# A v tile computed ahead of a stall, and the q and k projections one step earlier, in a sliding-window attention kernel

## The chip, the cores and the metric

The kernel runs on one core of a Trainium2 chip. The metric is the device time of one execution in microseconds (us). A core has engines that work side by side: PE (TensorE, matmuls), DVE (VectorE), ACT (ScalarE), POOL (GpSimd) and SP (SyncE); in the kernel before PE is busy 99% of the span, DVE 46%, ACT 31% and POOL 23%. SP computes nothing here: it issues DMA transfers, in its timelines one after the other, and among them all 102 DMA transposes of the trace. POOL and ACT issue DMAs too, beside their other work. The page counts all transfers, 101.21 MB, on the core's 16 DMA engines.

Before the change, three runs gave a median of 1196.67 us.

## The reference, cut to what matters

Four layers run one after the other: attention, gated MLP, attention, gated MLP. Only the first attention is changed.

```
def _A_ref(x, wqkv, wo):                # x: 2048 x 576, 32 heads of 18, window of 8, dilation 2
    qkv = (x @ wqkv) ...                # q, k, v
    idx = pos[:, None] - off[None, :]   # position s sees s, s-2, ... s-14
    logits = einsum(q, kg) * scale;  attn = softmax(masked logits)
    o = einsum(attn, vg)
    return o @ wo
x = x + _A_ref(_layernorm(x), A_wqkv, A_wo)
x = x + _B_ref(_layernorm(x), ...)      # gated MLP, 4608 wide
... # the same two again
```

## The kernel before: the parts that count here

The attention walks over tiles of 112 queries, in 38 steps, two per tile (half of the heads each). `L_mm` makes the logits, `EXP` (ACT) the exponentials, `PV` the product with v. Other work is hung into a table of steps and runs after the step's `PV`: `VW` makes half a v tile, `PG` one q or k projection of 512 positions, `WO` half an output projection.

```
def PG(d, qk, cc, dve, queues=(nc.sync, nc.gpsimd)):
    ... 5 matmuls pp <- wqk, xnT; evac to stg ...
    # when both halves of stg are there: up to 8 moves of q/k rows, SBUF to SBUF
    for dst, src in moves:
        dma_rr[0] += 1
        self.dma(dst, src, eng=queues[dma_rr[0] % len(queues)])      # SP and POOL in turn

def PV(s):
    ... O_ps matmuls; DVE normalizes into o_t ...
    if hf == 1:                                                      # every odd step
        if t < NT - 2:
            nc.sync.dma_start_transpose(out=oT[:, :, c0:c0 + nq], in_=o_t[:nq, :])   # SP

def XST(i):   # store of the new residual, SP
    self.dma(self.xres[li][i * P:(i + 1) * P, :], tails[i]["x"][:])
def LN_T(i):  # transpose of the normalized rows for the next layer, SP
    self.ln_T(tails.pop(i)["xn"], i * P, P)
...
for k_, (d, qk, cc) in enumerate(pgs):                # 12 projections in steps 2 to 13
    at(2 + k_ if li == 0 else ..., PG, d, qk, cc, True)
for i in range(NS):
    t = -(-(i + 1) * P // QT) - 1                     # the last tile that WO(i) needs
    s = 2 * t + (6 if li == 0 and t < 10 else 5 if t < NT - 5 else 4 if t < NT - 3 else 3)
    at(s - 5, XO, i); at(s, WO, i, 0); at(s + 1, WO, i, 1)
    at(s + 1, LN_STATS, i); at(s + 2, LN_XN, i); at(s + 2, XST, i); at(s + 4, LN_T, i)   # (joined here)
...
for s in range(NST):
    if s + 1 < NST:
        L_mm(s + 1); EXP(s + 1)
    PV(s)
    for f, a in table.pop(s, []):
        f(*a)
```

Transpose `t` is put on SP's list in step 2t+1, and `WO(i)` reads it in step 2t+6 while t is under 10, and in step 2t+5 from t = 10 on.

The softmax here doesn't subtract the row's maximum and nothing guards it: scores larger than these inputs give would overflow.

Of the kernel before, what the change touches and what calls it, by code (L numbers as in the profile page):

```python
# [62 lines left out]
class K:  # L63
# [257 lines left out]
    def layer_A(self, li):  # L321
# [32 lines left out]
        def tdim(t):  # L354
            nq = min(QT, S - QT * t)
            return HALO + nq, nq
# [11 lines left out]
        def evac(out, in_, dve):  # L368
            if dve:
                nc.vector.tensor_copy(out=out, in_=in_)  # L370
            else:
                nc.scalar.copy(out=out, in_=in_)

        def VW(t, hh, dve):
            nk = tdim(t)[0]
            pv = self.PT_tile([P, 512], f32, "pv")
            for c in range(5):
                nc.tensor.matmul(pv[:nk, 0:288], lhsT=self.xnT[:, c, QT * t:QT * t + nk],  # L378
                                 rhs=wv_sb[:, c, hh * 288:(hh + 1) * 288], start=(c == 0), stop=(c == 4))
            evac(v_ext[:nk, t, 16 * hh:16 * hh + 16, 0:DH], pv[:nk, 0:288].rearrange("p (b d) -> p b d", d=DH), dve)  # L380
# [46 lines left out]
        def L_mm(s):  # L427
            t, hf = divmod(s, 2)
            nk, nq = tdim(t)
            L_tiles[s] = [self.H_tile("L_ps") for _ in range(2)]  # L430
            for jp in range(2):
                for ftl in range(4):
                    g = 4 * hf + ftl
                    for jj in range(2):
                        j = 2 * jp + jj
                        nc.tensor.matmul(L_tiles[s][jp][:nk, jj, ftl * QT:ftl * QT + nq],  # L436
                                         lhsT=kT[32 * j:32 * j + 32, g, QT * t:QT * t + nk],
                                         rhs=qT[32 * j:32 * j + 32, g, QT * t + PADL:QT * t + PADL + nq],
                                         start=True, stop=True, tile_position=(32 * j, 0))

        def EXP(s):
            nk, nq = tdim(s // 2)
            for jp, L_ps in enumerate(L_tiles.pop(s)):
                Lv = L_ps[:, :, 0:4 * QT].rearrange("p a (b c) -> p a b c", c=QT)
                nc.scalar.activation(out=P_bufs[(2 * s + jp) % 4][:nk, :, :, 0:nq], in_=Lv[:nk, :, :, 0:nq], func=ACT.Exp,  # L445
                                     scale=scale)

        def PV(s):
            t, hf = divmod(s, 2)
            nk, nq = tdim(t)  # L450
            O_ps = self.PT_tile([P, 512], f32, "O_ps")
            for jp in range(2):
                for ftl in range(4):
                    for jj in range(2):
                        idx = 4 * ftl + 2 * jp + jj
                        nc.tensor.matmul(O_ps[:, idx * (DH + 1):(idx + 1) * (DH + 1)],  # L456
                                         lhsT=P_bufs[(2 * s + jp) % 4][:nk, jj, ftl, :],
                                         rhs=v_ext[:nk, t, 16 * hf + idx, :], start=True, stop=True)
            Ov = O_ps[:, 0:16 * (DH + 1)].rearrange("p (h e) -> p h e", e=DH + 1)
            o_t = o_bufs[t % len(o_bufs)]  # L460
            rec = sb.tile([P, 16], f32, name="rec", tag="rec", bufs=2)
            nc.vector.reciprocal(out=rec[:nq, :], in_=Ov[:nq, :, DH])
            nc.vector.tensor_tensor(out=o_t[:nq, 288 * hf:288 * (hf + 1)].rearrange("p (h d) -> p h d", d=DH),
                                    in0=Ov[:nq, :, 0:DH], in1=rec[:nq, :, None].to_broadcast([nq, 16, DH]), op=ALU.mult)
            if hf == 1:
                c0 = (QT * t) % (RING * P)
                if t < NT - 2:
                    nc.sync.dma_start_transpose(out=oT[:, :, c0:c0 + nq], in_=o_t[:nq, :])
# [45 lines left out]
        if li == 0:  # L514
# [58 lines left out]
            def T_(*tiles):  # L573
                for i in tiles:
                    self.ln_T(xns.pop(i), i * P, P)
# [50 lines left out]
                    R_(12, 4)  # L626
                    A_(12, 13, 14, 15)
            T_(12, 13, 14, 15)
            nvw0, nvw = 4, 8
        else:  # L630
            for k_, (d, cc) in enumerate([(d, cc) for d in range(5) for cc in range(2)]):
                for qk in ((1, 0) if d < 4 else (0,)):
# [8 lines left out]
                if k_ == 6:  # L641
                    self.fill_window_rows(QK, 1)
            nvw0, nvw = 0, 4
        for t in range(nvw0, nvw):
            for hh in range(2):
                VW(t, hh, li == 0)

# [10 lines left out]
        def at(s, f, *a):  # L658
            table.setdefault(s, []).append((f, a))
        pgs = [(d, qk, cc) for d, cc in ((0, 2), (1, 2), (2, 2), (0, 3), (1, 3), (2, 3), (3, 2), (3, 3), (4, 2), (4, 3))  # L660
               for qk in ((1, 0) if d < 4 else (0,))]
        PG_END = 14
        pre, pgs = pgs[:6], pgs[6:]
        for k_, (d, qk, cc) in enumerate(pgs):
            at(2 + k_ if li == 0 else (k_ * PG_END) // len(pgs), PG, d, qk, cc, True)
        for t in range(nvw, NT):
            for hh in range(2):
                if li == 0 and t == nvw:
                    at(hh, VW, t, hh, True)
                else:  # L670
                    at(2 * t - 2 + hh, VW, t, hh, 2 * t - 2 + hh >= PG_END and hh == 0)
        for i in range(NS):
            t = -(-(i + 1) * P // QT) - 1
# [18 lines left out]
        for k_, (d, qk, cc) in enumerate(pre):  # L692
            if k_ == (2 if li == 0 else 0):
                L_mm(0)
                EXP(0)
            PG(d, qk, cc, li > 0 or k_ < 4, q2)
            if li == 0 and k_ == 3:
                self.fill_window_rows(QK, 1)
        for s in range(NST):
            if s + 1 < NST:  # L700
                L_mm(s + 1)
                EXP(s + 1)
# [3 lines that stand above are left out]
# [339 lines left out]
```

## Time and profile before

| what | value |
|---|---|
| time, median of 3 | 1196.67 us (1194.73 to 1196.80) |
| first matmul of layer 1 | 133.2 us |
| PE waits between 12 and 140 us | 4.5 us |
| cold clock (granted clock 0.50) in that stretch | 6.83 us from 47.63 us and 3.41 us from 92.00 us |

From the page of the kernel before, three lines: PE's busy tenths and the granted TensorE clock in 40 slices of the span, and the shares of the chain of work that ended last.

```profile
PE   9999999999999999999999999999999999999998
...
PEclk9899999999999999999999999999999999999999
...
PE 94%; DMA 2%; SPq 1%; POOL 1%; DVE 1%; issue 0%; ACT 0%; DVEq 0%; POOLq 0%
```

PE is busy nearly everywhere and is nearly the whole chain. The clock row has its gap in the second slice (30 to 60 us). So only a few microseconds in the first attention can be won by moving work. The waits view of the kernel before, for PE from 12 to 140 us, says who waited for what (us in sum, times, longest):

```profile
PE L_ps L436 <- DMA QK<-win2a: 2.0, 3, 1.0
PE L_ps L436 <- DMA QK<-stg: 1.6, 2, 1.5
PE L_ps L436 <- ACT P_sb L445: 0.9, 2, 0.4
```

The PE timeline of the kernel before shows where (start, length, instruction group; in brackets the idle time before it and what ended it):

```profile
46.65 0.20 PE L436 MATMUL L_ps<-QK 32*128 32x112 bf16 x1 [0.96 <-DMA QK<-win2a]
47.24 0.46 PE L436 MATMUL L_ps<-QK 32*128 32x112 bf16 x8 [0.39 <-DMA QK<-win2a]
48.38 0.27 PE L436 MATMUL L_ps<-QK 32*128 32x112 bf16 x1 [0.68 <-DMA QK<-win2a]
...
90.84 0.22 PE L436 MATMUL L_ps<-QK 32*128 32x112 bf16 x1 [1.45 <-DMA QK<-stg]
91.22 0.22 PE L436 MATMUL L_ps<-QK 32*128 32x112 bf16 x1 [0.16 <-DMA QK<-stg]
```

The logits of step 1 wait for the last q/k moves before the loop, from the buffer `win2a`, lent here, into `QK` ("stall 1", 46 to 48 us), and those of step 19 for the last moves of the loop ("stall 2", 89 to 91 us). The windows view of the kernel before, cut every 3.41 us for a reason given below it, has the length first, then busy us of PE, PEld, DVE, ACT and POOL, then the granted clock, the DMA share and GB/s:

```profile
44.22:47.63 3.41, 2.06 (x21) 0.88 (x19) 3.41 (x4) 1.30 (x3) 3.28 (x4) 1.00 1.14 185
47.63:51.04 3.41, 2.73 (x46) 1.66 (x46) 2.17 (x4) 1.76 (x3) 2.73 (x4) 0.50 1.05 336
51.04:54.46 3.42, 3.42 (x54) 2.01 (x52) 1.71 (x5) 2.89 (x4) 0.00 (x0) 0.50 1.03 362
88.60:92.00 3.40, 1.79 (x38) 1.16 (x37) 1.59 (x7) 2.10 (x4) 3.03 (x3) 1.00 0.35 72
92.00:95.42 3.42, 3.42 (x44) 2.09 (x43) 1.77 (x5) 1.11 (x2) 3.23 (x5) 0.50 0.93 243
```

After the window of stall 1 (PE busy 2.06 of 3.41 us) the clock is 0.50 for two windows, after that of stall 2 (1.79 of 3.40 us) for one. The packed trace has a record of each stretch of granted clock. In the kernel before, from the first record (6.67 us) to the end of the span, these stretches are 1.00 or 0.50 and last 40.96, 6.83, 37.55, 3.41 and 1099.09 us, each within 2 ns of a whole multiple of 3.4133 us (12, 2, 11, 1 and 322 times). That is why the views are cut every 3.41 us.

SP's list is full (from 58 us). In SP's timeline the four moves that stall 2 waits for (85.38 us) are issued behind a transpose of oT (83.32 us). The last line is the transpose of tile 10, which the output projection `WO(8,0)` reads. In the PE timeline it is the second half of this group:

```profile
108.09 1.39 PE L493 MATMUL pw<-wo_sb,oT 128*128 128x288 bf16 x10
```

Five of these ten matmuls are `WO(7,1)` and five are `WO(8,0)`, which thus begins near 108.7 us: 5.5 us after its transpose began to be issued. It did not wait. The packed trace also holds the semaphore updates that tell when a transfer has landed, which `prof` does not list for these transposes. By them this one landed at 108.11 us, 4.9 us after its issue began. So it was 0.6 us in time.

### The profile page before, as it was taken

What the parts mean: (1) busy time and instruction counts of PE and PEld (TensorE: products, weight loads), DVE (VectorE), ACT (ScalarE), POOL (GpSimd) and SP (SyncE); (2) the same over time, 40 slices, a digit from 0 to 9 for tenths busy, and PEclk for the clock granted to TensorE, in tenths of its full rate; (3) what the DMA queues carried; (4) which work ended last, traced back from release to release, by engine and by line L of the source; (5) the groups of instructions that cost most, each with busy time, mean ns of one, the idle gap of its engine ahead of it and who ended that gap; (6) DMA issues with size and microseconds to landing.
All of it is one profiled execution on the core that took longest, in us unless ns stands there. A gap on an engine that the chain in (4) does not pass through costs nothing.

```text
span 1193.7 us, 20761 instructions
## 1 busy us (share of the span) xinstructions
PE 1182.4 (99%) x8554; PEld 621.8 (52%) x8554; DVE 548.0 (46%) x1207; ACT 376.0 (31%) x592; POOL 275.3 (23%) x383
## 2 busy tenths in 40 slices
PE   9999999999999999999999999999999999999998
PEld 5566644444444444457755775444444444444677
DVE  9687677333233233244455776763223223223311
ACT  6477677211111111201156786770110110111000
POOL 4677773100000000001144777530000000000000
PEclk9899999999999999999999999999999999999999
DMA  8989892000000000049646899900000000000332
GB/s 198 190 160 220 166 221 67 23 1 12 12 12 12 12 1 12 2 139 297 169 97 111 190 236 186 224 11 12 12 12 1 12 12 12 12 1 25 127 105 73
DMA packets 178103, 101.21 MB, mean 85 GB/s; under 512 B 134335, under 2 KB 159359, under 8 KB 178008
## 3 DMA queue, kind: packets, MB, share of 16 engines
q1 hardware_dynamic: 165144, 78.13, 30.9%
q0 software_dynamic: 6512, 16.00, 5.2%
q10 hardware_dynamic: 6352, 5.75, 1.6%
q8 instruction: 67, 1.10, 0.4%
q14 instruction: 28, 0.23, 0.1%
HBM read 42.39 MB, written 16.53 MB: 49 GB/s over the span
## 4 chain that ended last, share of the span: by engine, by line
PE 94%; DMA 2%; SPq 1%; POOL 1%; DVE 1%; issue 0%; ACT 0%; DVEq 0%; POOLq 0%
PE pg L879 42%; PE pz L861 12%; PE po L933 12%; PE pz L783 11%; PE pp L401 4%; PE pw L493 3%; PE pv L378 3%; PE O_ps L456 3%; PE L_ps L436 2%; PE pzs L783 1%; SPq L77 1%; DMA QK<-win2a 1%; POOL QK L77 1%; DMA oT<-o_t 1%; DMA oT<-in_A_x_dram 1%
## 5 line engine op out<-in xcount | busy, mean ns | idle before, releaser
L879 PE MATMUL pg<-Wq,Z 128*128 128x512 bf16 x2304 | 502.8, 379 | 0.0
L879 PEld LDWEIGHTS <-Z 128*128 128x128 bf16 x2304 | 225.5, 98 | 271.7
L883 DVE TENSOR_TENSOR g_tmp<-pg,ln_xn 128x512 f32<-128x512 f32 x144 | 99.5, 691 | 428.9 <-PE pg L879 428.9
L873 ACT ACTIVATE z1T<-pz 128x1024 bf16<-128x1024 f32 x72 | 73.7, 1023 | 513.9 <-PE pz L861 513.7
L77 POOL DMA_DIRECT2D wout<-in_B_w_out_dram x4 | 4.2, 1062 | 604.6 <-PE pg L879 604.6
L445 ACT ACTIVATE P_sb<-L_ps 128x896 bf16<-128x896 f32 (+1 forms) x152 | 126.9, 888 | 46.6 <-PE L_ps L436 46.3
L933 PE MATMUL po<-wout,Z 128*128 128x288 bf16 x1152 | 141.4, 286 | 0.0
L861 PE MATMUL pz<-xnT,w 128*128 128x512 bf16 (+1 forms) x640 | 136.0, 380 | 0.0
L933 PEld LDWEIGHTS <-Z 128*128 128x128 bf16 x1152 | 112.7, 98 | 28.8
L783 PEld LDWEIGHTS <-xnT 128*128 128x128 bf16 (+1 forms) x800 | 66.3, 97 | 80.9 <-issue 23.7
L783 PE MATMUL pz<-win2a,xnT 128*128 128x512 bf16 x384 | 104.8, 380 | 0.0
L884 DVE TENSOR_TENSOR Z<-g_tmp,z1T 128x512 bf16<-128x512 f32 x144 | 99.6, 692 | 10.1 <-DVE g_tmp L883 0.5
L861 PEld LDWEIGHTS <-w 128*128 128x128 bf16 (+1 forms) x640 | 51.1, 97 | 80.0 <-issue 27.1
L401 PE MATMUL pp<-xnT,wqk_sb 128*128 128x512 bf16 x360 | 82.9, 380 | 0.0
L797 ACT ACTIVATE zp<-pz 128x1024 bf16<-128x1024 f32 x64 | 65.5, 1023 | 36.8 <-PE pz L783 34.2
L241 POOL TENSOR_SCALAR ln_xn<-x_new,ln_mv,ln_rstd 128x576 bf16<-128x576 f32 x32 | 73.3, 2290 | 3.0
L943 DVE TENSOR_TENSOR x_new<-po,xo 128x288 f32<-128x288 f32 (+1 forms) x64 | 28.8, 455 | 87.9 <-PE po L933 83.9
L783 PE MATMUL pz<-win2b,xnT 128*128 128x512 bf16 (+1 forms) x256 | 65.8, 380 | 0.0
L799 DVE CUSTOM_DVE_ANT_0 Z<-zp 128x1536 bf16<-128x1536 bf16 x32 | 56.3, 1760 | 16.1 <-ACT zp L797 16.0
L77 POOL DMA_DIRECT2D QK<-stg x81 | 50.7, 631 | 39.0 <-DVE stg L370 23.6
L378 PE MATMUL pv<-wv_sb,xnT 128*128 128x288 bf16 (+1 forms) x380 | 57.6, 291 | 0.0
L401 PEld LDWEIGHTS <-wqk_sb 128*128 128x128 bf16 x360 | 33.3, 98 | 36.1 <-issue 0.5
(112 smaller groups left out, 892.1 us busy)
## 6 DMA issues: line engine op xcount, KB each, us to landing
xres<-x_new SPq DMA_DIRECT2D x48, 288.0 KB
xo<-xres SPq DMA_DIRECT2D x32, 288.0 KB
wout<-in_B_w_out_dram POOLq DMA_DIRECT2D x4, 1296.0 KB, 8.4
xo<-xres SPq DMA_DIRECT2D x8, 576.0 KB
w<-in_B_w_in_dram SPq DMA_DIRECT2D x16, 256.0 KB
QK<-stg POOLq DMA_DIRECT2D x53, 72.0 KB, 4.1
QK<-stg SPq DMA_DIRECT2D x41, 72.0 KB
xo<-in_A_x_dram SPq DMA_DIRECT2D x8, 288.0 KB
```

The source lines that it names most:

```text
L77: return eng.dma_start(out=out, in_=in_)
L241: e.tensor_scalar(out=xn[:nrows, 0:D], in0=x_t[:nrows, :], scalar1=mv[:nrows, 0:1], scalar2=rstd[:nrows, 0:1], op0=ALU.subtract, op1=ALU.mult)
L378: nc.tensor.matmul(pv[:nk, 0:288], lhsT=self.xnT[:, c, QT * t:QT * t + nk], rhs=wv_sb[:, c, hh * 288:(hh + 1) * 288], start=(c == 0), stop ...
L401: nc.tensor.matmul(pp[:, :], lhsT=w, rhs=self.xnT[:, c, PADL + cc * 512:PADL + (cc + 1) * 512], start=(c == 0), stop=(c == 4))
L445: nc.scalar.activation(out=P_bufs[(2 * s + jp) % 4][:nk, :, :, 0:nq], in_=Lv[:nk, :, :, 0:nq], func=ACT.Exp, scale=scale)
L783: nc.tensor.matmul(pzvs[ci][:, sub * 512:sub * 512 + w], lhsT=self.xnT[r0:r1, c, PADL + i * P:PADL + (i + 1) * P], rhs=win2(c)[r0:r1, c0 + ...
L861: nc.tensor.matmul(pz1s[q // 2][:, q % 2, :], lhsT=w1[r0:r1, c, sub * P:(sub + 1) * P], rhs=self.xnT[r0:r1, c, PADL + q * 512:PADL + (q + ...
L873: nc.scalar.activation(out=z1T[:, q2 * 512:(q2 + 2) * 512], in_=pz1s[q2 // 2][:, :, :].rearrange("p a b -> p (a b)"), func=ACT.Gelu_apprx_ ...
L879: nc.tensor.matmul(pg[:, :], lhsT=Z[:, jj, i, sub * P:(sub + 1) * P], rhs=Wq[q][:, i, :], start=(i == 0), stop=(i == NS - 1))
L883: nc.vector.tensor_tensor(out=tmp[:], in0=pg[:, :], in1=bsp[:, qs], op=ALU.add)
L884: nc.vector.tensor_tensor(out=uT(jj)[:, sub, qs], in0=tmp[:], in1=z1Ts[jj, sub][:, qs], op=ALU.mult)
L933: nc.tensor.matmul(acc[hh], lhsT=uT(j // 2)[:, j % 2, i * P:(i + 1) * P], rhs=wouts[j // NJH][:, j % NJH, hh * 288:(hh + 1) * 288], start= ...
```

## The change

The intent is to put PE work into stall 1 and to bring the last q/k moves forward, out of stall 2. One v tile more is computed ahead: both halves of tile 8 run before the second logits. Step 0 then gets half of tile 9, and its other half goes to step 13. The 12 projections of the loop run in steps 1 to 12, not 2 to 13.

```
-            nvw0, nvw = 4, 8
+            nvw0, nvw = 4, 9
...
-        for t in range(nvw0, nvw):
+        for t in range(nvw0, nvw - (1 if li == 0 else 0)):
             for hh in range(2):
                 VW(t, hh, li == 0)
...
-            at(2 + k_ if li == 0 else (k_ * PG_END) // len(pgs), PG, d, qk, cc, True)
+            at(1 + k_ if li == 0 else (k_ * PG_END) // len(pgs), PG, d, qk, cc, True)
...
                 if li == 0 and t == nvw:
-                    at(hh, VW, t, hh, True)
+                    at(13 * hh, VW, t, hh, True)
...
+        if li == 0:
+            VW(nvw - 1, 0, False)
+            VW(nvw - 1, 1, False)
         for s in range(NST):
```

## The prediction

> **What bounds the kernel.** TensorE: the page has PE busy 99% of the span, 94% of the chain that ended last. The change touches the first attention (layer 0, to about 133 us). The windows view of 0 to 135 us shows 7.0 us without a matmul and a mean clock of 0.96; from 135 to 600 us there is none, at clock 1.00. What can be won lies in two stalls and what they do to the clock.
>
> *Stall 1.* In the PE timeline the logits of step 1 start at 45.4 us and wait for "DMA QK<-win2a" 0.96 + 0.39 + 0.68 = 2.0 us, until 48.4 us: the last q/k move (d = 4, first half). In small windows the clock is 0.50 from 47.6 to 54.5 us.
>
> *Stall 2.* The logits of step 19 wait 1.6 us at 89.4 us for "DMA QK<-stg", the moves of step 13's projection. It is evacuated by 81.1 us, but the SP queue, full from 58 us on, issues its four moves at 85.4 to 88.5 us, behind a 2.0 us transpose; POOL issues its four at 82.4 us, behind a layer norm. They land at 91.2 us. The clock is 0.50 from 92.0 to 95.4 us.
>
> The cold stretches are two and one times 3.41 us. [...] here 1.35 us (PE busy 2.06 of 3.41) and 1.6 us (1.79 of 3.40) without matmuls sufficed.
>
> **What the change does.** Nothing is removed. Two halves of v tile 8 (0.61 us each at full clock) go from steps 0 and 1 (cold: 1.21 us each) into stall 1, where PE waits anyhow. Step 0 gets half of tile 9; its other half goes from step 17 to 13. Each projection (1.09 us) runs a step earlier, and its moves fall in even steps: ahead of the odd step's transpose on SP and of that step's layer norm on POOL.
>
> **Costs.**
> - Work moved into stall 1: -1.2 to -1.6 us, certain. The last move still lands at 48.4 us; some 0.9 us of waiting is left.
> - Cold clock after stall 1: 48.6 to 55.3 us would take 5.4 us warm, not 6.6: -1.25 us, at 75%.
> - Stall 2: SP issues the last moves about 5 us earlier, PE arrives 2 to 3 us earlier: -1.6 us, at 85%.
> - Cold clock after stall 2: -1.5 us, at 85%.
> - Against it: steps 14 to 17 lose v halves and become bound by ACT (two exponentials, 1.73 us a step): +0.3 us.
>
> Sum about -5 us. PE is continuous from 92 us far into layer 1, so the gain reaches the end. Layers 1 to 3 are unchanged.
>
> **Predicted: 1191.8 us, 80% range 1189.3 to 1194.6.** Faster by over 2%: 0.5%; within: 99%; slower: 0.5%.
>
> **Right if:** tile 8's pv matmuls lie at 45.3 to 46.5 us; the wait for QK<-win2a is below 1.2 us; the clock stays 1.00 at 48 to 55 us; the wait for QK<-stg near 87 us is below 0.3 us, with clock 1.00 after it; layer 1's first matmul (133.2 us) comes at about 128 us; later stages keep their lengths.
>
> **Wrong if:** the waiting that is left still drops the clock[...]; SP's backlog still delivers the last moves late, since PE arrives earlier; the earlier moves collide with the win2a load (DMA share 1.0 at 49 to 55 us) and hold up middle steps; ACT binds more steps.

No term of the sum is cut: the author put it at about -5 us. Its cold and warm times can be read from the trace: in the kernel before, the matmuls of a v tile start 0.240 us apart at clock 0.50 (49.2 to 50.0 us) and 0.122 us apart at 1.00 (85.5 to 86.0 us), which makes 1.20 and 0.61 us for the five of a half. The -1.25 us for the cold clock after stall 1 are the estimate from such times.

## More of the kernel before

The timeline of SP for the kernel before: each line is the issue of DMAs, not their transfer.

```profile
83.32 1.97 SPq L468 DMA_TRANSPOSE oT<-o_t  x1
85.38 3.10 SPq L77 DMA_DIRECT2D QK<-stg  x4
...
98.73 1.22 SPq L468 DMA_TRANSPOSE oT<-o_t  x1
100.04 1.97 SPq L248 DMA_TRANSPOSE xnT<-ln_xn  x1
102.11 0.53 SPq L77 DMA_DIRECT2D xres<-x_new  x1
102.69 0.43 SPq L77 DMA_DIRECT2D xo<-in_A_x_dram  x1
103.22 1.35 SPq L468 DMA_TRANSPOSE oT<-o_t  x1
```

## The result, and the profile after

The changed kernel took 1197.84 us in the median of four runs (1195.84 to 1200.68), the kernel before 1195.89 us. The ratio is 1.0019, 95% interval 0.9995 to 1.0043. Ratios here are the mean time of one kernel's fast runs over that of the other's fast runs of the same rounds, so they are not quite the ratio of the medians. In two later sets of six runs, on two chips, the changed kernel came to 1.0000 and 1.0002. No gain arrived, and 1197.84 us is outside the predicted range of 1189.3 to 1194.6 us.

Single runs of one kernel differ by up to 8 us (1191.76 to 1199.51 us in 11 runs of the kernel before, in e1's record), so profiles must be read with care: each is one run, and that of the changed kernel is the fastest of its four (1195.84 us). The page of the changed kernel (same lines as before) shows that the clock's gap went from the second slice to the fourth (90 to 119 us):

```profile
PEclk9998999999999999999999999999999999999999
...
PE 95%; DMA 2%; POOL 1%; DVE 1%; ACT 1%; issue 1%; DVEq 0%; ACTq 0%
```

The waits view of the changed kernel, PE, 12 to 140 us:

```profile
PE pw L493 <- DMA oT<-o_t: 4.3, 2, 3.4
...
PE L_ps L436 <- DMA QK<-win2a: 0.5, 1, 0.5
```

The wait for the moves of stall 2 is gone, and that of stall 1 is down from 2.0 to 0.5 us. In their place the output projections (pw) wait 4.3 us for oT, which cost nothing before. Its PE timeline:

```profile
45.51 1.39 PE L378 MATMUL pv<-wv_sb,xnT 128*128 128x288 bf16 x10
...
48.44 0.22 PE L436 MATMUL L_ps<-QK 32*128 32x112 bf16 x1 [0.50 <-DMA QK<-win2a]
...
89.02 0.79 PE L493 MATMUL pw<-wo_sb,oT 128*128 128x288 bf16 x5 [0.91 <-DMA oT<-o_t]
...
107.52 1.38 PE L493 MATMUL pw<-wo_sb,oT 128*128 128x288 bf16 x5 [3.40 <-DMA oT<-o_t]
```

Tile 8's matmuls are where they were meant to be (45.51 us, ten of them). At 89 us a pw waits 0.91 us; at 107.52 us `WO(8,0)` waits 3.40 us. The windows of the changed kernel, columns as before:

```profile
47.63:51.04 3.41, 2.91 (x65) 1.95 (x61) 2.68 (x7) 2.69 (x4) 2.97 (x5) 1.00 1.11 332
88.60:92.00 3.40, 2.98 (x57) 2.15 (x59) 2.05 (x6) 1.88 (x4) 2.90 (x5) 1.00 0.75 176
103.50:106.90 3.40, 0.63 (x6) 0.27 (x3) 1.72 (x6) 0.99 (x2) 0.86 (x2) 1.00 1.11 149
106.90:110.30 3.40, 2.78 (x40) 1.71 (x41) 0.73 (x3) 0.81 (x1) 2.23 (x2) 0.52 1.09 277
110.30:113.70 3.40, 3.40 (x44) 2.05 (x43) 2.10 (x6) 1.67 (x3) 0.00 (x0) 0.50 0.46 132
```

The first two show what was predicted: the clock stays at 1.00 where it was 0.50 or about to fall. The third is the new wait, with PE busy 0.63 of 3.40 us, and behind it two cold windows (0.52 and 0.50; by the clock's record 6.83 us at 0.50 from 107.02 us). SP's timeline has the transposes concerned:

```profile
79.48 3.10 SPq L77 DMA_DIRECT2D QK<-stg  x4
...
84.67 1.23 SPq L468 DMA_TRANSPOSE oT<-o_t  x1
...
101.06 1.98 SPq L468 DMA_TRANSPOSE oT<-o_t  x1
```

The last moves (79.48) now begin 5.9 us sooner. The transpose of tile 6 (84.67) is issued behind them and 1.35 us later than before, that of tile 10 (101.06) is only 2.2 us sooner. The critical view of the changed kernel, 84 to 115 us, has the time of both from the start of their issue to their landing:

```profile
84.67 4.30 DMA oT<-o_t
...
101.06 6.42 DMA oT<-o_t
```

So tile 10 took 6.4 us, of which 1.98 us were its issue, and landed at 107.48 us. Before the change it took 4.9 us.

How far PE was ahead of the kernel before, from the starts of PV in the two PE timelines, tells where the gain went:

| start of PV of step | before, us | after, us | ahead, us |
|---|---|---|---|
| 0 | 48.59 | 48.59 | 0.00 |
| 4 | 57.78 | 56.41 | 1.37 |
| 13 | 78.71 | 77.34 | 1.37 |
| 17 | 87.27 | 85.34 | 1.93 |
| 18 | 91.37 | 86.92 | 4.45 |
| 25 | 107.06 | 102.32 | 4.74 |
| 26 | 109.74 | 109.35 | 0.39 |
| 28 | 114.03 | 115.17 | -1.14 |
| first matmul of layer 1 | 133.24 | 134.31 | -1.07 |

(Only from step 18 on have both kernels done the same work: by step 4 the changed one has run half a v tile and one projection more, 0.61 + 1.09 us.) By step 25 PE was 4.7 us ahead although it had already waited 0.91 us for oT. From step 25 to 28 the changed kernel took 12.85 us, the one before 6.97 us. Of the 5.9 us of difference, 3.4 us are the wait itself, and the other 2.5 us fall in the cold windows behind it. In this profile that cancels the gain.

### The profile page after: what moved, and what is told of

Same layout as the page of the kernel before. It is cut to its first block, busy times and chain, and to the rows that moved or that the text cites. A ratio compares the mean times of both kernels' runs of the same rounds, so it can differ in the third digit from the quotient of the medians.

```text
span 1194.1 us, 20758 instructions
## 1 busy us (share of the span) xinstructions
PE 1181.1 (99%) x8554; PEld 620.7 (52%) x8554; DVE 547.6 (46%) x1206; ACT 376.5 (32%) x593; POOL 276.9 (23%) x383
## 4 chain that ended last, share of the span: by engine, by line
PE 95%; DMA 2%; POOL 1%; DVE 1%; ACT 1%; issue 1%; DVEq 0%; ACTq 0%
PE pg L882 42%; PE pz L864 12%; PE po L936 12%; PE pz L786 11%; PE pp L401 5%; PE pw L493 3%; PE pv L378 3%; PE O_ps L456 3%; PE L_ps L436 2%; PE pzs L786 1%; DMA oT<-o_t 1%; POOL QK L77 1%; ACT P_sb L445 0%; DMA QK<-stg 0%; DMA QK<-win2a 0%
## 5 line engine op out<-in xcount | busy, mean ns | idle before, releaser
L493 PE MATMUL pw<-wo_sb,oT 128*128 128x288 bf16 x320 | 50.0, 291 | 4.3 <-DMA oT<-o_t 4.3
```

The source lines that it names most:

```text
L493: nc.tensor.matmul(pw[:, 0:288], lhsT=oT[:, c, r0:r0 + P], rhs=wo_sb[:, c, hh * 288:(hh + 1) * 288], start=(c == 0), stop=(c == 4))
```

## The experiments

Theory SP: between 58 and 108 us the list of SP is the limit. SP issues q/k moves, stores, loads and two kinds of transposes in one order. PE had been slow enough, thanks to its own stalls, for the oT transposes to come in time. A faster PE meets them. What speaks for it is SP's track above, which is nearly solid with issues (45.8 of 50 us). The rivals: the new order on SP is at fault, not its load (ORDER); the 16 DMA engines are full (busy share 0.93 over the same 50 us in the kernel before) and SP isn't (DMA); it is only where the clock's steps of 3.413 us fall in a run (CLOCK). They do fall differently: the clock drops at 47.63 us in the kernel before and at 107.02 us in the changed one, 3.26 and 1.20 us past a multiple of 3.4133 us, counted from the first instruction.

Every experiment ran in five rounds and gave six times; kernels of a group shared a chip and 11 runs of the kernel before. All gave correct results. "Waits" are those of PE in the one profiled run.

| group | kernel | mean us | ratio to before | 95% interval | mean clock |
|---|---|---|---|---|---|
| 1 | before (11 runs) | 1195.14 | | | 0.9969 |
| 1 | e1_after | 1195.26 | 1.0000 | 0.9976 to 1.0024 | 0.9982 |
| 1 | e2_v_only | 1194.47 | 0.9992 | 0.9969 to 1.0015 | 0.9970 |
| 1 | e3_proj_only | 1195.63 | 1.0003 | 0.9980 to 1.0026 | 0.9970 |
| 1 | e4_wo_later | 1191.10 | 0.9965 | 0.9943 to 0.9987 | 0.9995 |
| 2 | before (11 runs) | 1196.11 | | | 0.9975 |
| 2 | e5_xst_act | 1193.77 | 0.9981 | 0.9965 to 0.9998 | 0.9985 |
| 2 | e6_pool_moves | 1194.42 | 0.9987 | 0.9966 to 1.0008 | 0.9982 |
| 2 | e7_win2b_late | 1196.22 | 1.0002 | 0.9983 to 1.0020 | 0.9982 |
| 2 | e8_sp_tiny | 1200.37 | 1.0036 | 1.0020 to 1.0053 | 0.9953 |
| 3 | before (11 runs) | 1195.21 | | | 0.9975 |
| 3 | e9_act_moves | 1192.90 | 0.9981 | 0.9964 to 0.9998 | 0.9988 |
| 3 | e10_margin_only | 1192.80 | 0.9983 | 0.9965 to 1.0001 | 0.9980 |
| 3 | e11_wo_later_2 | 1191.99 | 0.9973 | 0.9957 to 0.9990 | 0.9992 |
| 3 | e12_win2a_spread | 1192.96 | 0.9981 | 0.9965 to 0.9998 | 0.9983 |
| 4 | before (11 runs) | 1195.71 | | | 0.9975 |
| 4 | e13_first_later | 1192.61 | 0.9974 | 0.9956 to 0.9992 | 0.9998 |
| 4 | e14_margin_v | 1193.42 | 0.9983 | 0.9964 to 1.0002 | 0.9980 |
| 4 | e15_margin_2 | 1192.97 | 0.9977 | 0.9959 to 0.9995 | 0.9988 |
| 4 | e16_wo_later_3 | 1191.51 | 0.9965 | 0.9947 to 0.9983 | 0.9992 |
| 5 | before (11 runs) | 1195.47 | | | 0.9975 |
| 5 | e17_after_3 | 1195.01 | 1.0002 | 0.9982 to 1.0022 | 0.9978 |
| 5 | e18_both_relief | 1192.42 | 0.9976 | 0.9955 to 0.9998 | 0.9988 |

The means are of all runs of a kernel, the ratios of those of the same rounds; so for e17 the quotient of the means (0.9996) is not quite the ratio.

### e1_after: the changed kernel again

No edit.

> The changed kernel again, unedited, in five rounds. Theory SP (the SP queue, which issues the oT transposes, is the limit between 60 and 108 us, so that what TensorE wins before 89 us it waits for at the output projections): ratio to the kernel before 0.999 to 1.003, and in the profile again waits of the pw matmuls for oT of about 3 to 5 us in sum, with a 0.50 clock after the longest. Rival CLOCK[...]: waits of under 1 us for oT in this run and a time 3 us off the first one.

It equals the kernel before. Its profile has the waits for oT, but smaller, and a new one. From its waits view:

```profile
PE pp L401 <- DMA xnT<-ln_xn: 4.9, 1, 4.9
PE pw L493 <- DMA oT<-o_t: 2.2, 2, 1.4
```

A third wait of pw (0.98 us), which the profile puts down to PE, ended 0.09 us after its oT had landed by the semaphore updates; with it the sum is 3.2 us. The first projection of step 1 (pp) waited 4.9 us for xnT, the transposed input of the last tiles, also issued by SP. In the kernel before that projection ran in step 2. This is a second place where work moved forward meets a transpose. The expectation did not name it. SP's list is not the reason here: it issued the last of these transposes at 45.7 us in this run as in the first profile of the changed kernel, but it landed after 9.2 us (at 54.94 us), not 4.3. The rival CLOCK, as the only cause, does not fit, since the waits for oT are over 1 us again and the run lost its time to waits.

### e2_v_only: the v tile alone

```
 (changed kernel)
-            at(1 + k_ if li == 0 else ..., PG, ...)
+            at(2 + k_ if li == 0 else ..., PG, ...)
-                    at(13 * hh, VW, t, hh, True)
+                    at(hh, VW, t, hh, True)
```

> Only the v tile goes ahead of the second logits; projections stay in steps 2 to 13. Theory SP: stall 1 is cut to under 1.2 us and the clock stays 1.00 after it, but SP still issues the last q/k moves near 85 to 88 us, so the logits of step 19 wait for QK<-stg longer than the 1.6 us of the kernel before, 3 to 5 us; time within 1.5 us of the kernel before. Rival WORK (the 1.2 us of moved work is kept wherever PE is continuous): 1.2 to 4 us faster than the kernel before.

The time is that of the kernel before within the noise, as theory SP said. But the interval reaches down to 0.9969 (3.7 us faster), so it does not exclude WORK, and most of what the theory named did not show. The PE timeline of e2:

```profile
48.88 0.43 PE L436 MATMUL L_ps<-QK 32*128 32x112 bf16 x2 [1.45 <-DMA QK<-win2a]
...
90.39 0.22 PE L436 MATMUL L_ps<-QK 32*128 32x112 bf16 x1 [0.38 <-DMA QK<-stg]
91.19 0.22 PE L436 MATMUL L_ps<-QK 32*128 32x112 bf16 x1 [0.58 <-DMA QK<-stg]
```

Stall 2 was 0.38 + 0.58 us, not 3 to 5: in this run stall 1 left a wait of 1.45 us and the clock fell all the same (0.83 over 40 to 60 us), so PE was not early. Only SP's late issue of the last moves (86.65 us) came as expected.

### e3_proj_only: the earlier projections alone

```
 (kernel before)
-            at(2 + k_ if li == 0 else ..., PG, ...)
+            at(1 + k_ if li == 0 else ..., PG, ...)
-                    at(hh, VW, t, hh, True)
+                    at(13 * hh, VW, t, hh, True)
```

> Only the projections run a step earlier (v tile 8 stays in the loop: one half in step 0, the other in step 13). Theory SP: stall 1 and its cold clock stay, stall 2 is gone; PE arrives at the output projections some 2 to 3 us later than in the changed kernel, so their waits for oT are under 2 us; 0 to 3 us faster than the kernel before. Rival ORDER (the new order of moves and transposes on SP is itself what delays the oT transposes): waits for oT of over 3 us also here, and a time of 1 us or more over the kernel before.

Stall 2 is gone, and a pw waits 1.7 us near 107 us. The profile puts that wait down to DVE (ln_rstd), but by the semaphore updates the oT that it reads landed at 107.08 us and the matmul began at 107.12, so it is a wait for oT. No gain in the mean. With the wait under 2 us ORDER gets no support, and with a time equal to the kernel before neither theory's number is clear of the noise.

### e4_wo_later: the change, with the output projections one step later

```
 (changed kernel)
-            s = 2 * t + (6 if li == 0 and t < 10 else 5 if t < NT - 5 else ...)
+            s = 2 * t + (7 if li == 0 and t < 10 else 6 if li == 0 and t < 12 else 5 if t < NT - 5 else ...)
```

> The changed kernel, with the output projections of tiles up to t = 11 one step later. SP and DMA do the same work. Theory SP (and a rival in which the DMA engines themselves are full): the transposes are late by 1 to 4 us only against a fixed step, one step is 1.7 to 2.2 us, so the waits for oT fall from 4.3 us to under 1.5 us, the clock stays 1.00, and the kernel is 2 to 5 us faster than the kernel before. Rival THROUGHPUT (SP can't finish its list before 110 us whatever the order): the wait moves to later steps with the same sum, and the time equals that of the changed kernel within 1 us.

It is 0.35% faster than the kernel before, about 4 us, and the interval is clear of 1. Its waits view, PE, 12 to 140 us:

```profile
PE L_ps L436 <- ACT P_sb L445: 0.9, 3, 0.3
PE L_ps L436 <- DMA QK<-win2a: 0.7, 1, 0.7
```

No wait for oT, the clock 1.00 all through the first 140 us, and layer 1's first matmul at 127.1 us, where the prediction wanted it (about 128 us). SP and the DMA engines did the same work. So the rival THROUGHPUT is out: the transposes were late, not impossible to deliver. But the edit does two things. It gives the transposes a step more, and it puts the stores and the transposes for the next layer, which hang on `WO`, a step later on SP's list. SP issued tile 10's transpose at 97.09 us, 4.0 us before the changed kernel, and it landed at 101.44 us. By an estimate from this trace it would have been in time even in step 25, whose projection `WO(7,0)` began at 101.53 us. Which of the two removes the wait was not separated. This is the version that beats both kernels; two repeats (e11, e16) gave 0.9973 and 0.9965.

### e5_xst_act: stores issued by ACT

```
 (changed kernel, XST)
-            self.dma(self.xres[li]..., tails[i]["x"][:])
+            self.dma(self.xres[li]..., tails[i]["x"][:], eng=nc.scalar if li == 0 else None)
```

> The changed kernel, with layer 0's stores of the residual (one of 288 KB of f32 per tile, 0.55 us of issue on SP each) issued by ACT in place of SP: the same transfers, less work for SP. Theory ISSUE (SP's time to issue, one after the other, is what delays the oT transposes): SP's list is 0.65 us shorter per tile, some 4 to 5 us by step 25, so the waits for oT fall to under 1.5 us in the profile and the time falls by 1.5 to 4 us against the changed kernel, less what ACT loses. Theory DMA (the 16 engines are full, share about 1.0 at 84 to 112 us): the same bytes, so the same waits of 3 us or more and the same time within 1 us.

```profile
PE pw L493 <- DMA oT<-o_t: 1.6, 1, 1.6
```

The wait for oT (line above, from its waits view) is under that of the changed kernel in its first profile (4.3 us) and under that of the second (2.2 us in the view, 3.2 us with the third wait); the wait for ACT rose from 0.8 to 1.8 us. The mean is 2.3 us under the kernel before. It goes the way of ISSUE, short of its 1.5 us.

### e6_pool_moves: more moves from POOL

```
 (changed kernel)
-            at(1 + k_ ..., PG, d, qk, cc, True)
+            at(1 + k_ ..., PG, d, qk, cc, True, *((q2,) if li == 0 and d < 3 else ()))   # q2 = POOL, SP, POOL
```

> The changed kernel, with two in three (not one in two) of the q/k moves of d = 0 to 2 in the steps issued by POOL, which is idle for half of 57 to 71 us. Theory ISSUE: SP has about 4 moves of 0.8 us less before step 8; it comes to the oT transposes earlier, the waits for oT fall by 1 to 3 us. Theory DMA: no change.

The wait for oT was 1.9 us; the mean is 1.7 us under the kernel before and not clear of it. Inconclusive by itself.

### e7_win2b_late: less DMA load in the stretch

```
 (changed kernel)
-        at(PG_END + 2, alloc_win2b)          ... at(PG_END + 2 + 2 * k_, win2b_piece, k_)
+        at(PG_END + 12, alloc_win2b)         ... at(PG_END + 12 + k_, win2b_piece, k_)      # layer 0 only
```

> The changed kernel, with layer 0's loads of win2b (1.03 MB of the 6.17 MB of 84 to 112 us, issued by POOL) moved from steps 16 to 26 to steps 26 to 31. SP issues what it did. Theory DMA: transposes land sooner, the waits for oT at steps 18 and 25 fall by half or more. Theory ISSUE: they stay within 1 us of the 4.3 us and 2.2 us of the two profiles of the changed kernel.

Its waits view has two lines with pw:

```profile
PE pw L493 <- DMA oT<-o_t: 1.8, 1, 1.8
PE pw L493 <- DVE ln_st L217: 1.2, 1, 1.2
```

Each is the wait of an output projection, 3.0 us in sum. The second, which the profile puts down to DVE, is at 121.4 us and ended 0.05 us after its oT had landed by the semaphore updates. The time equals the kernel before. Yet this does not put DMA out. The transposes of tiles 6 to 11 took 2.9 us on average from issue to landing, against 4.3, 4.1 and 4.0 us in the three profiles of the changed kernel (after, e1, e17). And the new wait lies where the moved loads now run: tile 14's transpose, the one that it waited for, took 6.7 us there, against 3.4 to 4.8 us. So the loads, not only SP's list, seem to make transposes late; moving them moved a wait. It is one profile.

### e8_sp_tiny: more issues for SP, no bytes

```
 (kernel before)
+        if li == 0:
+            tiny = main.tile([1, 23 * 16], bf16, name="tiny")
+            for k_ in range(23):
+                at(2 + k_, self.dma, tiny[:, k_ * 16:(k_ + 1) * 16], self.A_x[0:1, k_ * 16:(k_ + 1) * 16], nc.sync)
```

> The kernel before, with one more DMA of 32 bytes issued by SP in each of steps 2 to 24 (into a tile that nobody reads). Nearly no bytes, about 0.4 us of SP's time each. Theory ISSUE: SP, full from 58 us on, falls behind by up to 9 us; the wait of the logits of step 19 grows over 1.6 us or waits for oT appear, together over 3 us, and the kernel is 2 to 8 us slower. Theory DMA: no change over 1 us.

```profile
PE pw L493 <- DMA oT<-o_t: 2.6, 1, 2.6
PE L_ps L436 <- DMA QK<-stg: 2.4, 4, 0.9
```

The kernel before with 23 loads of 32 bytes more on SP is 0.36% (4.3 us) slower, clear of the noise. Its waits view (above) now has the wait for oT, which the profile of the kernel before does not have, and a longer one for the last moves: 5.0 us in sum, against 1.6 us. This is the cleanest result for ISSUE: with 736 bytes more the DMA engines were not busier (share 0.67, 0.75 and 0.86 in the three stretches of 20 us from 60 to 120 us, in the kernel before 0.92, 0.86 and 1.16), but 23 more entries delay SP's list; those that stand alone in its timeline took SP 0.27 to 0.43 us each. The transpose of tile 10 took no longer (4.0 us to landing, 4.9 us in the kernel before), but its issue began at 108.11 us, not at 103.22.

### e9_act_moves and e12_win2a_spread: relief for the transposes of the input

```
 (e9: e4, moves of d = 4 before the loop)
-   PG(d, qk, cc, False, (nc.gpsimd, nc.sync) if d in (0, 4) else q2)
+   PG(d, qk, cc, False, (nc.gpsimd, nc.sync) if d == 0 else (nc.gpsimd, nc.scalar) if d == 4 else q2)
 (e12: e4, the six loads of win2a)
-   for f in reversed(self.load_win2a(nc.gpsimd)):
-       at(0, f)
+   for k_, f in enumerate(reversed(self.load_win2a(nc.gpsimd))):
+       at(3 + 2 * k_, f)
```

> The changed kernel with the later output projections of e4_wo_later, and with the q/k moves of d = 4, first half, shared by POOL and ACT (idle at 34 to 41 us) in place of POOL and SP. SP then comes some 3 us earlier to the last four transposes of the input (xnT), for which the first projection of step 1 waited 4.9 us in one profile of the changed kernel. Theory ISSUE: no wait of pp for xnT, stall 1 no longer, spread of the six runs smaller; 0 to 1.5 us faster than e4. Rival: the late xnT is a matter of the DMA engines alone; then nothing moves.

> e4_wo_later, with the six pieces of the win2a load (1.77 MB, needed at 127 us) issued in steps 3, 5, ... 13 in place of all in step 0 (45 to 50 us), where they run beside the last q/k moves and the transposes of xnT. Theory DMA for the wait for xnT and the rest of stall 1: DMA share at 45 to 56 us falls, xnT and QK land sooner, no wait of pp for xnT, 0 to 1.5 us faster than e4 with a smaller spread. Theory ISSUE for these: as e4, within 0.7 us; POOL's issue time (0.85 us a piece) may delay the q/k moves of the steps a little.

Neither had a wait for xnT in its profile, and stall 1 was 0.2 us in e9. But both were some 0.9 us slower in the mean than e11, the same kernel without them, on the same chip, which is within the noise. No use could be shown.

### e10_margin_only, and e11, e15, e16: is it the margin alone?

e10 and e15 have only e4's line for `s`, on the kernel before. e11 and e16 are e4 unedited.

> The kernel before with only the later output projections (no v tile ahead, projections in steps 2 to 13). Its profile showed no wait for oT, so the margin has nothing to take away: ratio to the kernel before 0.999 to 1.001, stalls 1 and 2 as before. Rival: the later output projections are good by themselves (fuller steps 14 to 17 or fewer waits); then it is 2 us or more faster, and the gain of e4 is not the change's.

> e4_wo_later again, unedited, on this chip, to be compared with the other three: 2.5 to 5 us faster than the kernel before, no waits for oT over 0.5 us.

> e10 again on this chip: later output projections alone. Stall 1 as in the kernel before (0.5 to 2 us, in some runs with a cold clock after it), no stall 2, because SP has one layer norm's transpose and store less ahead of the last q/k moves: 1 to 3 us faster than the kernel before.

> e4 again on this chip: 2.5 to 4.5 us faster than the kernel before, 0.8 to 2.5 us faster than e15 if the change is worth its 1.2 us of moved work and some cold clock with the margin in place; within 0.5 us of e15 if it is not.

The expectation of e10 was wrong: the margin alone gains 0.17% and 0.23% (the first interval just reaches 1, the second is clear of it). SP's timeline of e10 shows a likely reason:

```profile
81.31 3.09 SPq L77 DMA_DIRECT2D QK<-stg  x4
```

The last q/k moves are issued at 81.3 us, not 85.4, because the stores and the transposes for the next layer hang on the output projections and come a step later too, behind these moves. Neither e10 nor e15 shows stall 2. The margin thus does a part of what the change was for. The whole change on top of it (e11 against e10, e16 against e15) is 0.8 and 1.5 us faster in the mean: 1.1 us on average, with an uncertainty of about 1.4 us (from the spread of the four sets of six). That the change is worth something beside the margin is likely and not shown.

### e13_first_later and e14_margin_v

```
 (e13: e4)
-            at(1 + k_ if li == 0 else ..., PG, ...)      -    at(13 * hh, VW, t, hh, True)
+            at(max(2, 1 + k_) if li == 0 else ..., PG, ...)   +    at(hh, VW, t, hh, True)
 (e14: e2 with e4's line for s)
```

> e4 with the second half of v tile 9 in step 1 and two projections in step 2, so that no projection runs before step 2 and the last still runs in step 12. If the wait of the first projection for xnT (4.9 and 0.8 us in two of five profiles) is a second loss: 0.3 to 1.5 us faster than e16 in the mean and no wait of pp for xnT over 0.3 us. Rival: it is rare and costs nothing on average: the same as e16 within 0.5 us.

> Later output projections and the v tile ahead of the second logits; projections in steps 2 to 13. If the v tile's gain is real once transposes have a margin: stall 1 at 0.5 to 0.8 us, clock 1.00 after it; but PE then comes to step 19 earlier than in e15 and waits 0.5 to 2 us for QK<-stg: 0 to 1.5 us faster than e15, 0 to 2 us slower than e16. Rival (the change is worth nothing beyond the margin): all three within 0.5 us.

e13 had no wait for xnT in the loop, but its mean is 1.1 us over e16; its profiled run has a wait of 2.4 us at 102.6 us that the profile puts down to o_t. That the xnT wait costs time on average could not be shown this way. (The "two of five profiles" in its expectation is a miscount; it was two of ten.) e14 lies with e15, within the noise: the v tile alone adds nothing visible to the margin.

### e17_after_3 and e18_both_relief: SP relieved, margin as in the change

e18 is the changed kernel with the edits of e5 and e6 together.

> The changed kernel, unedited, as the control of e18 on the same chip: within 1.5 us of the kernel before in the mean; in the profile waits of pw for oT of 2 to 5 us in sum.

> The changed kernel, output projections where the change has them, with both reliefs of SP: stores of layer 0 from ACT (e5) and two in three of the moves of d = 0 to 2 from POOL (e6). The same bytes. Theory ISSUE: the waits of pw for oT fall under 1.5 us in sum and the mean is 1.5 to 4 us under e17. Theory DMA (the transposes take their time on the engines, whoever issues the rest): waits of 2 us or more and a mean within 1 us of e17.

The waits views of the two, first e17:

```profile
PE pw L493 <- DMA oT<-o_t: 2.4, 2, 1.8
...
PE pp L401 <- DMA xnT<-ln_xn: 0.6, 1, 0.6
```

and e18:

```profile
PE pp L401 <- DMA xnT<-ln_xn: 2.5, 1, 2.5
...
PE pw L493 <- DMA oT<-o_t: 0.9, 1, 0.9
```

The wait for oT is 0.9 us, under the 1.5 that ISSUE set, and the mean is 2.6 us under e17. With six runs each, which spread by 2 to 3 us, that difference is not clear of the noise; against the kernel before, e18 is clear (0.9976, up to 0.9998). Its profiled run was the longest of the six (1196.08 us) and has another wait for xnT (2.5 us). That spoils the reading of the 0.9 us: PE was held up before it came to the output projections, and even so tile 10's transpose, issued at 102.14 us, landed at 108.77 us, 0.2 us before its use. So the profile does not show that the relief brought the transposes in time. Over all profiles with a projection in step 1, 4 of 13 have a wait for xnT (0.6 to 4.9 us).

## Why the prediction was wrong

- *Stall 1 cut, "-1.2 to -1.6 us, certain", and the cold clock after it, -1.25 us.* Right in the profile of the result: 0.5 us of wait left (0.9 forecast), clock 1.00. But not in every run: e2 and e11 kept 1.45 and 0.71 us of wait and went cold (0.50 from about 50.4 and 49.9 us). Of the 15 profiles with the v tile ahead, 7 have a stretch at 0.50 between 45 and 60 us, in e1 and e18 after the wait for xnT.
- *Stall 2, -1.6 us, and its cold clock, -1.5 us.* Right: the wait is gone and the clock at 88.6 to 92 us stays 1.00. SP issued the last moves 5.9 us sooner, against "about 5".
- *The sum, about -5 us.* By step 25 PE was 4.74 us ahead and had waited 0.91 us for oT, so in this profile the terms together brought some 5.6 us. They were the right size.
- ***"PE is continuous from 92 us far into layer 1, so the gain reaches the end."*** This is the step that failed. PE was continuous there in the old trace because it came late. The chain of waits shows what did hold PE up, and nothing of how near the next transfer was. The transpose of tile 10 landed 0.6 us before its use. In the changed kernel PE came to that use 4.6 us sooner (ready at 104.12 us, not 108.70), SP issued the transpose only 2.2 us sooner, and it took 1.5 us longer to land (6.4 us, not 4.9): 4.6 - 2.2 + 1.5 - 0.6 = 3.3 us, which is nearly the wait of 3.40 us. The new waits (0.91 + 3.40 us) and 2.5 us lost around the cold windows took 6.8 us.
- *"SP's backlog still delivers the last moves late" was listed as a way to be wrong.* The right queue, the wrong entry on it: the moves went first, and the transposes came late.
- *Not seen at all:* the first projection moved to step 1 can come before xnT does (4.9 us in e1). How often, and what it costs on average, stays open.

That SP's time to issue delays the transposes is shown in one direction by e8 (more entries, no bytes: 4.3 us slower, with the waits in the expected places). The time of e18 (fewer entries, same bytes) points the same way and is not clear of its control. e7 points to a second part, the load of the DMA engines, in the time to landing. So the missing margin is measured, but how much of the lateness is SP's list and how much the load stays open. e4 shows that one step of margin, with the order of SP's list that comes with it, removes the wait.

## What to carry to other kernels

Before work is moved forward, look at every transfer that the faster engine will meet later, not only at those it waits for now: measure how long before its use each is issued and how long it takes to land. A queue that is full in the trace need not keep up with a faster consumer: here SP, full from 58 us on, came 2.2 us sooner where PE came 4.6 us sooner. What is won upstream of it can become a wait downstream, and with it a cold clock (here 3.40 us, and 6.83 us at 0.50). Here one constant, which sets the steps between a transpose and its use and with them the order on SP's list, turned a change worth nothing (1.0000, 1.0002) into one of 0.3% (0.9965, 0.9973, 0.9965), but that constant alone was already worth about 0.2%.

## What these runs show of the clock and of SP's list

- The clock was 0.50 after windows with 2.06 of 3.41 us and 1.79 of 3.40 us of matmuls, that is after 1.35 and 1.6 us without any (kernel before). A wait of 0.91 us did not drop it in the changed kernel: counted back in steps of 3.413 us from its clock change at 107.02 us, PE was busy 2.50 of 3.41 us (86.54 to 89.95), at 1.00. A wait of 0.70 us in e4 didn't either (PE busy 3.30 of 4 us from 46 us, clock 1.00 to 56 us), but one of 0.71 us in e11 (3.29 of 4 us) was followed by 0.50 from about 49.9 us. Nor does the busy time alone decide: e7 stayed at 1.00 (100 to 120 us) with 1.94 of 3.41 us busy (100.78 to 104.19), in a wait of 1.79 us. No busy share at which the clock drops can be given from these runs.
- Here the issue of a transfer was not small beside the transfer: the transposes of tiles 6 and 10 in the changed kernel took 1.23 and 1.98 us of SP's time out of 4.30 and 6.42 us from issue to landing, and 23 loads of 32 bytes on SP cost the kernel 4.3 us (e8).
- A full list on SP showed no wait at all on PE's side in the kernel before (no wait for oT), and still took back 4.7 us of lead in the changed one.
